# First batch of a cross-covariance attention with a max-out network: norms of q by one-column matmuls, and A^T W in parts of 128, 256 and 384 columns

One core of a Trainium2 chip. The metric is the device time of one execution in microseconds (us); lower is better.

## The reference

```python
# q, k, v: (4, 6144, 256), tau = 1
qn = q / (norm(q, axis=1) + 1e-6);  kn = k / (norm(k, axis=1) + 1e-6)
a = softmax(kn.transpose(0, 2, 1) @ qn / tau, axis=-1)     # (4, 256, 256)
x = (v @ a).reshape(24576, 256)
h = max(x @ w1, x @ w2, x @ w3)                            # d_ff = 768
out = h @ w_out
```

The product of q and k, q^T k, is called the gram. The kernel folds the small matrix A of each batch into the weights: it makes A^T W for three W once per batch ("ew products"), so that x is never formed. Then it works through 48 chunks of 512 rows of v: six "h blocks" of six matmuls each, a maximum of three on ACT and DVE, and the "o products" with the output weights.

## The kernel before

What the change and the argument touch (cuts marked):

```python
    def gram(b):                       # first batch only
        # ... k^T k for the norms of k while k lands ...
        for tp in range(NG // 2):
            for j in range(CC):
                PE.matmul(ps[j][:, 0:C], lhsT=qt[:, tsl, jsl], rhs=kt[:, tsl, :], ...)        # q^T k
                PE.matmul(ps[j][:, C:C + P], lhsT=qt[:, tsl, jsl], rhs=qt[:, tsl, jsl], ...)  # q^T q

    def softmax_t(ps, rkb):            # norm of q: the diagonal of q^T q
        for j in range(CC):
            DVE.tensor_tensor_reduce(out=scr, in0=ps[j][:, C:C + P], in1=ident, ..., accum_out=n2q[:, j:j + 1])
        # ... Ln, Exp, scaling, Exp ...

    # the loads, in this order on one queue: q, then
    load_v(0)
    for fp in range(d_ff // FT):       # FT = 256 columns
        load_w(fp)
    load_v(1)

    # the start of the program
    ps = gram(0)
    # ... six warm matmuls (on zeros, their result is not read) ...
    et = softmax_t(*ps)
    v_transpose_pe(0)                  # chunk 0 of v by PE
    rinv = aw_first(et, aw)            # columns 0:256 of A^T W
    v_transpose(1)                     # chunk 1 of v by a DMA transposition
    hold_loads(1)                      # POOL waits until that has landed
    POOL.dma_start(out=wo_sb, ...)     # only now: the output weights
    # ... chunk 0: h block 0, columns 256:512, h blocks 1 and 2, columns 512:768, h blocks 3 to 5
    # ... chunk 1: h block 0, h block 1, then the first o products (they read wo_sb)
```

## Time and profile before

574.09 us median of 4 runs (574.03 to 574.11).

| what | value | how to read it |
|---|---|---|
| span | 572.1 us | first to last instruction |
| PE, DVE, ACT, POOL busy | 97, 72, 54, 41% | PE is the bound over the whole |
| PE in 40 slices | below 9 tenths in the first two and the last | the start and the end are all there is to gain |

The lines of the chain and of the timeline that carry the start stand in the prediction. These are lines of the timeline of the kernel before (start, length, engine, line):

```profile
42.19 10.85 SPq L365 DMA_TRANSPOSE vt_sb<-v_sb  x2
...
45.36 0.83 POOL L483 DMA_DIRECT2D wo_sb<-in_moe_w_out_dram  x1
...
50.63 0.82 PE L409 MATMUL o_ps<-wo_sb,ht_sb 128*128 128x256 bf16 x6
```

and this is the answer for the tile of the output weights:

```profile
DMA to landing us min/median/max: 5.2/5.2/5.2
```

Chunk 1 of v lands and its transposition starts at 42.19; when that is done, POOL issues the output weights at 45.36; they land 5.2 us later (the landing event of the trace is at 50.54). The first o matmul starts at 50.63. PE did not wait, so no view of waits names this load. But it landed only 0.09 us ahead of its use.

### The profile page before, as it was taken

How to read it: one execution, taken by the hardware profiler on the slowest of the kernel's cores; microseconds unless marked ns; L12 is line 12 of the kernel's file. 1: busy time of each engine (PE TensorE's matmuls, PEld its weight loads, DVE VectorE, ACT ScalarE, POOL GpSimd, SP SyncE). 2: the span in 40 equal slices, each digit the busy share in tenths (PEclk: the TensorE clock that was granted, in tenths of full speed). 3: DMA queues.
4: the chain of work that ended last, by engine and by line, in shares of the span. 5: the costliest groups of instructions: out<-in, count | busy, mean ns of one | idle time of the engine just before them, and what ended most of it. 6: DMA issues, size and time to landing. Idle time of an engine off the chain costs nothing.

```text
span 572.1 us, 9442 instructions
## 1 busy us (share of the span) xinstructions
PE 553.9 (97%) x3349; PEld 330.7 (58%) x3350; DVE 411.1 (72%) x647; ACT 309.1 (54%) x539; POOL 235.1 (41%) x240
## 2 busy tenths in 40 slices
PE   3799999999999999999999999999999999999997
PEld 2665555555755555555575555555575555555566
DVE  0048777877577777777768777777868778778775
ACT  1044567677454576776545467767645444444443
POOL 2443357776730078776560048777750000000000
PEclk9999999999999999999999999999999999999999
DMA  9998998884598168984179339885437323132112
GB/s 143 106 146 129 136 237 126 159 135 116 99 107 160 56 107 158 134 148 110 57 128 151 99 81 140 148 141 98 124 86 154 75 75 109 56 103 64 56 55 76
DMA packets 76960, 65.64 MB, mean 115 GB/s; under 512 B 52464, under 2 KB 62576, under 8 KB 76784
## 3 DMA queue, kind: packets, MB, share of 16 engines
q0 software_dynamic: 19072, 26.48, 38.7%
q1 hardware_dynamic: 57696, 38.41, 23.7%
q8 instruction: 26, 0.43, 0.3%
q14 instruction: 22, 0.18, 0.1%
q10 hardware_dynamic: 144, 0.13, 0.1%
HBM read 78.64 MB, written 25.17 MB: 181 GB/s over the span
## 4 chain that ended last, share of the span: by engine, by line
PE 93%; DMA 5%; POOL 0%; issue 0%; DVE 0%; POOLq 0%
PE h_ps L389 65%; PE o_ps L409 22%; DMA q_sb<-in_q_dram 5%; PE gram L260 3%; PE ew_ps L311 3%; POOL k_sb L99 0%; PE o_ps L434 0%; PE ew_ps L335 0%; PE warm_ps L469 0%; PE vt_ps L372 0%; PE gram L177 0%; PE n_ps L215 0%; DVE ht_sb L395 0%; DVE o_sb L461 0%; PE n_ps L217 0%
## 5 line engine op out<-in xcount | busy, mean ns | idle before, releaser
L389 PE MATMUL h_ps<-vt_sb,aw_sb 128*128 128x512 bf16 (+1 forms) x1764 | 406.7, 375 | 0.1
L389 PEld LDWEIGHTS <-aw_sb 128*128 128x128 bf16 x1764 | 171.8, 98 | 161.3 <-DVE aw_sb L317 2.0
L394 DVE TENSOR_TENSOR s_mx<-h_ps,s_mx 128x512 bf16<-128x512 f32 (+1 forms) x294 | 198.7, 676 | 87.1 <-ACT s_mx L393 86.8
L393 ACT ACTIVATE s_mx<-h_ps 128x512 bf16<-128x512 f32 (+1 forms) x294 | 172.4, 587 | 124.9 <-PE h_ps L389 124.0
L395 DVE TENSOR_TENSOR ht_sb<-h_ps,s_mx 128x512 bf16<-128x512 f32 (+1 forms) x294 | 200.2, 681 | 31.4 <-PE o_ps L409 0.5
L203 POOL TENSOR_TENSOR acc<-acc,sq 128x768 f32<-128x768 f32 x90 | 147.6, 1651 | 70.5 <-ACT sq L197 61.6
L409 PE MATMUL o_ps<-wo_sb,ht_sb 128*128 128x256 bf16 x1128 | 153.9, 273 | 0.0
L409 PEld LDWEIGHTS <-ht_sb 128*128 128x128 bf16 x1128 | 110.4, 98 | 52.0
L412 ACT ACTIVATE o_sb<-o_ps 128x512 f32<-128x512 f32 x94 | 56.1, 597 | 85.3 <-PE o_ps L409 85.3
L110 POOL DMA_DIRECT2D v_sb<-in_v_dram x48 | 27.5, 578 | 37.7 <-DMA vt_sb<-v_sb 35.5
L197 ACT ACTIVATE sq<-q_sb 128x768 bf16<-128x768 fp8e4 x48 | 40.5, 845 | 0.0
L197 ACT ACTIVATE sq<-k_sb 128x768 bf16<-128x768 fp8e4 x48 | 40.1, 835 | 0.0
L200 POOL CAST acc<-sq 128x768 f32<-128x768 bf16 x6 | 4.9, 823 | 68.7 <-ACT sq L197 68.7
L102 POOL DMA_DIRECT2D q_sb<-in_q_dram x33 | 18.4, 564 | 5.1 <-DMA v_sb<-in_v_dram 4.1
L165 PE MATMUL kk<-k_sb 128*128 128x256 fp8e4 x48 | 7.5, 338 | 11.9 <-DVE k_sb L151 6.3
L99 POOL DMA_DIRECT2D k_sb<-in_k_dram x29 | 16.1, 555 | 3.1 <-DMA v_sb<-in_v_dram 1.2
L260 PE MATMUL gram<-k_sb,q_sb 128*128 128x512 fp8e4 x144 | 16.8, 277 | 0.0
L260 PEld LDWEIGHTS <-q_sb 128*128 128x256 fp8e4 x144 | 15.9, 136 | 0.6
L314 ACT ACTIVATE aw_sb<-ew_ps,rinv 128x384 bf16<-128x384 f32 (+1 forms) x24 | 13.2, 555 | 5.5 <-PE ew_ps L311 4.7
L311 PE MATMUL ew_ps<-w_sb,et 128*128 128x384 bf16 (+1 forms) x96 | 15.6, 313 | 0.0
L177 PE MATMUL gram<-k_sb,q_sb 128*128 128x512 fp8e4 x48 | 11.4, 332 | 2.6 <-DMA q_sb<-in_q_dram 2.4
L165 PEld LDWEIGHTS <-k_sb 128*128 128x256 fp8e4 x48 | 6.4, 182 | 12.9 <-DMA k_sb<-in_k_dram 6.6
(67 smaller groups left out, 112.9 us busy)
## 6 DMA issues: line engine op xcount, KB each, us to landing
out_dram<-o_sb SPq DMA_DIRECT2D x41, 512.0 KB, 2.9
v_sb<-in_v_dram POOLq DMA_DIRECT2D x48, 256.0 KB, 4.2
k_sb<-in_k_dram POOLq DMA_DIRECT2D x24, 192.0 KB, 6.0
q_sb<-in_q_dram POOLq DMA_DIRECT2D x24, 192.0 KB, 7.6
out_dram<-o_sb SPq DMA_DIRECT2D x13, 256.0 KB, 2.0
k_sb<-in_k_dram POOLq DMA_DIRECT2D x5, 256.0 KB, 10.8
w_sb<-in_moe_w_dram POOLq DMA_DIRECT2D x9, 128.0 KB, 5.7
kf<-in_k_dram SPq DMA_DIRECT2D x1, 1024.0 KB, 4.8
```

The lines of the kernel that those rows point to most:

```text
L102: POOL.dma_start(out=qk[b][0][:, g0:g0 + w, :], in_=q_r[b][:, g0:g0 + w, :])
L110: POOL.dma_start(out=t, in_=v_r[gi // NCH, gi % NCH])
L197: ACT.activation(out=sq, in_=src, func=AF.Square)
L203: POOL.tensor_tensor(out=acc, in0=acc, in1=sq, op=ALU.add)
L260: PE.matmul(g[:, j * C:(j + 1) * C], lhsT=qt[:, tsl, j * P:(j + 1) * P], rhs=kt[:, tsl, :], start=(tp == 0 and j == 0), stop=(tp == NG // ...
L311: PE.matmul(ew[:, :w], lhsT=et[:, j, ic * P:(ic + 1) * P], rhs=w_sb[m][:, j, fsl], start=(j == 0), stop=(j == CC - 1))
L389: PE.matmul(t.rearrange("p (t n) -> p t n", n=P), lhsT=aw[m][:, ic, fsl], rhs=vt[:, tsl, ic, :], start=(ic == 0), stop=(ic == CC - 1))
L393: ACT.activation(out=s_mx, in_=hp[0], func=AF.Copy)
L394: DVE.tensor_tensor(out=s_mx, in0=hp[1], in1=s_mx, op=ALU.max)
L395: DVE.tensor_tensor(out=ht, in0=hp[2], in1=s_mx, op=ALU.max)
L409: PE.matmul(st["ps"][:, half], lhsT=ht[:, fc, t * P:(t + 1) * P], rhs=wo_sb[:, fc, :], start=(fc == 0), stop=(fc == FC - 1))
L412: ACT.activation(out=st["o"][:, t - 1:t + 1, :].rearrange("p t d -> p (t d)"), in_=st["ps"], func=AF.Copy)
```

## The change

Its intent is to shorten the string of dependences between the last piece of q and the first h matmul. The norms of q come from squares (half on ACT, half on DVE), summed by matmuls against a column of ones. The first part of A^T W is half as wide, the second part is made inside the first h block, and the weights are loaded in the same parts. Chunk 0 of v goes through two PSUM banks instead of one, and there are two warm matmuls instead of six. Cut to its core:

```diff
-                PE.matmul(ps[j][:, C:C + P], lhsT=qt[:, tsl, jsl], rhs=qt[:, tsl, jsl], ...)
+            ACT.activation(out=a[:, 0:h, :], in_=ra, func=AF.Square)
+            DVE.tensor_tensor(out=d[:, 0:h, :], in0=rd, in1=rd, op=ALU.mult)
+                    PE.matmul(nq[:, j:j + 1], lhsT=t[:, r, j * P:(j + 1) * P], rhs=ones_c, ...)
...
-    FT = 2 * P
+    PARTS = ((0, P), (P, 3 * P), (3 * P, d_ff))
...
+        sums(0)
         products(0, (0, 1))
-        sums(0)
         sums(1)
-        DVE.reciprocal(out=rinv, in_=rs_ps[:, 0:CC])
         products(1, (0, 1))
         for j in range(CC):
             products(j, (2,))
+        DVE.reciprocal(out=rinv, in_=rs_ps[:, 0:CC])
...
+    def h_block_first(aw, et, rinv):     # for each m: two h matmuls, then four ew products of PARTS[1]
...
-    for i in range(6):
+    for i in range(2):                   # warm matmuls
...
-                    for fp in range(1, d_ff // FT):
-                        gaps[2 * fp - 2].append(lambda fp=fp: aw_part(et, rinv, aw, fp, FT))
+                    gaps[2].append(lambda: aw_part(et, rinv, aw, *PARTS[2]))
```

More of the change, by code (lines that the diff above doesn't have):

```diff
@@ L75 @@
     sq_pool = ctx.enter_context(tc.tile_pool(name="sq", bufs=4))
+    sqq_pool = ctx.enter_context(tc.tile_pool(name="sqq", bufs=3))
     sm = ctx.enter_context(tc.tile_pool(name="sm", bufs=2))
@@ L118 @@
     SP.dma_start(out=kf, in_=k_r[0][:, 0:HEAD, :])
-    for load, widths in ((load_k, [8] * 5), (load_q, [8] * 4 + [4, 4, 4, 2, 2])):
+    QW = [8] * 4 + [4, 4, 4, 2, 2]
+    for load, widths in ((load_k, [8] * 5), (load_q, QW)):
         g0 = HEAD if load is load_k else 0
@@ L128, with load_w @@
     w_sb = [consts.tile([P, CC, d_ff], BF16, name=f"w{i}_sb") for i in range(3)]
-    FT = 2 * P
-    def load_w(fp):
-        fsl = slice(fp * FT, (fp + 1) * FT)
+    PARTS = ((0, P), (P, 3 * P), (3 * P, d_ff))
+    def load_w(lo, hi):
         for wt, w in zip(w_sb, w_list):
-            POOL.dma_start(out=wt[:, :, fsl], in_=w.rearrange("(cc p) f -> p cc f", p=P)[:, :, fsl])
+            POOL.dma_start(out=wt[:, :, lo:hi], in_=w.rearrange("(cc p) f -> p cc f", p=P)[:, :, lo:hi])
     load_v(0)
-    for fp in range(d_ff // FT):
-        load_w(fp)
+    for part in PARTS:
+        load_w(*part)
     load_v(1)
@@ L154, with gram_first @@
     neg_ln_tau = -math.log(float(tau)) if float(tau) != 1.0 else 0.0
-    def gram(b):
-        qt, kt = qk[b]
+    def gram_first():
+        qt, kt = qk[0]
         kk = htile("kk")
@@ L170, in gram, with squares, columns @@
             DVE.tensor_tensor(out=dkm[:, jsl], in0=kk[:, jsl], in1=ident, op=ALU.mult)
-        ps = [xtile(f"gram{j}") for j in range(CC)]
-        for tp in range(NG // 2):
-            tsl = slice(2 * tp, 2 * tp + 2)
-            last = tp == NG // 2 - 1
-            for j in range(CC):
-                jsl = slice(j * P, (j + 1) * P)
-                PE.matmul(ps[j][:, 0:C], lhsT=qt[:, tsl, jsl], rhs=kt[:, tsl, :],
-                          start=(tp == 0), stop=last, perf_mode=DR, skip_group_check=True)
-                PE.matmul(ps[j][:, C:C + P], lhsT=qt[:, tsl, jsl], rhs=qt[:, tsl, jsl],
-                          start=False, stop=last, perf_mode=DR, skip_group_check=True)
-            if tp == 11:
+        g = xtile("gram")
+        nq = htile("nq")
+        def squares(g0, w):
+            h = w // 2
+            a = sqq_pool.tile([P, QW[0] // 2, C], BF16, name="sqa")
+            d = sqq_pool.tile([P, QW[0] // 2, C], BF16, name="sqd")
+            ra, rd = qt[:, g0:g0 + h, :], qt[:, g0 + h:g0 + w, :]
+            ACT.activation(out=a[:, 0:h, :], in_=ra, func=AF.Square)
+            DVE.tensor_tensor(out=d[:, 0:h, :], in0=rd, in1=rd, op=ALU.mult)
+            return [(t, r) for t in (a, d) for r in range(h)]
+        def columns(rows, first=False, last=False):
+            for n, (t, r) in enumerate(rows):
+                for j in range(CC):
+                    PE.matmul(nq[:, j:j + 1], lhsT=t[:, r, j * P:(j + 1) * P], rhs=ones_c,
+                              start=(first and n == 0 and j == 0), stop=(last and n == len(rows) - 1),
+                              skip_group_check=True)
+        g0 = 0
+        rows = None
+        for i, w in enumerate(QW):
+            if rows:
+                columns(rows, first=(i == 1))
+            for tp in range(g0 // 2, (g0 + w) // 2):
+                tsl = slice(2 * tp, 2 * tp + 2)
+                for j in range(CC):
+                    PE.matmul(g[:, j * C:(j + 1) * C], lhsT=qt[:, tsl, j * P:(j + 1) * P], rhs=kt[:, tsl, :],
+                              start=(tp == 0 and j == 0), stop=(tp == NG // 2 - 1), perf_mode=DR,
+                              skip_group_check=True)
+            rows = squares(g0, w)
+            g0 += w
+            if i == 2:
                 kb_ps = htile("kb_ps")
@@ L187, in gram @@
                 ACT.activation(out=rkb, in_=lnk, func=AF.Exp, scale=-0.5)
-        return ps, rkb
+        columns(rows, last=True)
+        return [g[:, j * C:(j + 1) * C] for j in range(CC)], rkb, nq[:, 0:CC]
     SQW = 3
@@ L276, in exp_t, with softmax_first @@
         return et
-    def softmax_t(ps, rkb):
-        n2q = sm.tile([P, CC], FP32, name="n2q")
-        scr = sm.tile([P, P], FP32, name="scr")
-        for j in range(CC):
-            DVE.tensor_tensor_reduce(out=scr, in0=ps[j][:, C:C + P], in1=ident, scale=1.0, scalar=0.0,
-                                     op0=ALU.mult, op1=ALU.add, accum_out=n2q[:, j:j + 1])
+    def softmax_first(gs, rkb, n2q):
         lnq = sm.tile([P, CC], FP32, name="lnq")
@@ L287, in softmax_t @@
         ACT.activation(out=rq, in_=lnq, func=AF.Exp, scale=-0.5, bias=neg_ln_tau)
-        return exp_t(scaled([ps[j][:, 0:C] for j in range(CC)], rkb), rq)
+        return exp_t(scaled(gs, rkb), rq)
     def alloc_aw():
@@ L302, in rowsums, with product, evacuate, aw_part @@
         return rinv
-    def aw_part(et, rinv, aw, fp, w):
-        fsl = slice(fp * w, (fp + 1) * w)
-        n = 0
+    def product(et, ew, m, ic, lo, hi, js=range(CC)):
+        for j in js:
+            PE.matmul(ew[:, :hi - lo], lhsT=et[:, j, ic * P:(ic + 1) * P], rhs=w_sb[m][:, j, lo:hi],
+                      start=(j == 0), stop=(j == CC - 1))
+    def evacuate(rinv, aw, ew, m, ic, lo, hi):
+        dst, src, r = aw[m][:, ic, lo:hi], ew[:, :hi - lo], rinv[:, ic:ic + 1]
+        if ic == 0:
+            ACT.activation(out=dst, in_=src, func=AF.Copy, scale=r)
+        else:
+            DVE.tensor_scalar_mul(out=dst, in0=src, scalar1=r)
+    def aw_part(et, rinv, aw, lo, hi):
         for m in range(3):
@@ L309, in aw_part @@
                 ew = htile("ew_ps")
-                for j in range(CC):
-                    PE.matmul(ew[:, :w], lhsT=et[:, j, ic * P:(ic + 1) * P], rhs=w_sb[m][:, j, fsl],
-                              start=(j == 0), stop=(j == CC - 1))
-                if n % 2 == 0:
-                    ACT.activation(out=aw[m][:, ic, fsl], in_=ew[:, :w], func=AF.Copy,
-                                   scale=rinv[:, ic:ic + 1])
-                else:
-                    DVE.tensor_scalar_mul(out=aw[m][:, ic, fsl], in0=ew[:, :w],
-                                          scalar1=rinv[:, ic:ic + 1])
-                n += 1
+                product(et, ew, m, ic, lo, hi)
+                evacuate(rinv, aw, ew, m, ic, lo, hi)
     def aw_first(et, aw):
@@ L324, in aw_first @@
         rs_ps = xtile("rs_ps")
-        parts = [(m, ic, htile("ew_ps")) for m in range(3) for ic in range(CC)]
+        ews = [(m, ic, htile("ew_ps")) for m in range(3) for ic in range(CC)]
         def sums(j):
@@ L332, in products @@
         def products(j, ms):
-            for m, ic, ew in parts:
+            for m, ic, ew in ews:
                 if m in ms:
-                    PE.matmul(ew[:, :FT], lhsT=et[:, j, ic * P:(ic + 1) * P], rhs=w_sb[m][:, j, 0:FT],
-                              start=(j == 0), stop=(j == CC - 1))
+                    product(et, ew, m, ic, *PARTS[0], js=(j,))
+        sums(0)
         products(0, (0, 1))
-        sums(0)
         sums(1)
-        DVE.reciprocal(out=rinv, in_=rs_ps[:, 0:CC])
         products(1, (0, 1))
@@ L344, in aw_first @@
             products(j, (2,))
-        for n, (m, ic, ew) in enumerate(parts):
-            if n % 2 == 0:
-                ACT.activation(out=aw[m][:, ic, 0:FT], in_=ew[:, :FT], func=AF.Copy, scale=rinv[:, ic:ic + 1])
-            else:
-                DVE.tensor_scalar_mul(out=aw[m][:, ic, 0:FT], in0=ew[:, :FT], scalar1=rinv[:, ic:ic + 1])
+        DVE.reciprocal(out=rinv, in_=rs_ps[:, 0:CC])
+        for m, ic, ew in ews:
+            evacuate(rinv, aw, ew, m, ic, *PARTS[0])
         return rinv
@@ L369, in v_transpose_pe @@
         vt = vt_tile(gi)
-        vt_ps = xtile("vt_ps", cols=TPC * C, dtype=BF16)
-        for i in range(TPC * CC):
-            PE.matmul(vt_ps[:, i * P:(i + 1) * P], lhsT=v_sb[:, i * P:(i + 1) * P], rhs=ident,
-                      is_transpose=True, start=(i == 0), stop=(i == CC * TPC - 1))
-        half = TPC * CC // 2
-        ps = vt_ps.rearrange("p (i n) -> p i n", n=P)
-        DVE.tensor_copy(out=vt[:, half:, :], in_=ps[:, half:, :])
-        ACT.activation(out=vt[:, :half, :], in_=ps[:, :half, :], func=AF.Copy)
+        n = TPC * CC
+        cut = 6
+        banks = [xtile("vt_ps", cols=TPC * C, dtype=BF16), ps_h.tile([P, TPC * C], BF16, tag="h", name="vt_ps2")]
+        for b, (lo, hi) in enumerate(((0, cut), (cut, n))):
+            for i in range(lo, hi):
+                PE.matmul(banks[b][:, i * P:(i + 1) * P], lhsT=v_sb[:, i * P:(i + 1) * P], rhs=ident,
+                          is_transpose=True, start=(i == lo), stop=(i == hi - 1))
+        pa, pb = (t.rearrange("p (i n) -> p i n", n=P) for t in banks)
+        DVE.tensor_copy(out=vt[:, 0:cut, :], in_=pa[:, 0:cut, :])
+        ACT.activation(out=vt[:, cut:n, :], in_=pb[:, cut:n, :], func=AF.Copy)
     def h_block(gi, aw, fc, tsl=slice(0, TPC)):
@@ L395, in h_block @@
         DVE.tensor_tensor(out=ht, in0=hp[2], in1=s_mx, op=ALU.max)
+    def h_block_first(aw, et, rinv):
+        vt = vts[0]
+        hp = []
+        ews = []
+        for m in range(3):
+            t = htile(f"h_ps{m}")
+            for ic in range(CC):
+                PE.matmul(t.rearrange("p (t n) -> p t n", n=P), lhsT=aw[m][:, ic, 0:P], rhs=vt[:, :, ic, :],
+                          start=(ic == 0), stop=(ic == CC - 1))
+            hp.append(t)
+            ews.append([htile("ew_ps") for ic in range(CC)])
+            for ic in range(CC):
+                product(et, ews[m][ic], m, ic, *PARTS[1])
+        s_mx = mx_pool.tile([P, CHUNK], BF16, name="s_mx")
+        ht = hts[0][:, 0, :]
+        ACT.activation(out=s_mx, in_=hp[0], func=AF.Copy)
+        for ic in range(CC):
+            evacuate(rinv, aw, ews[0][ic], 0, ic, *PARTS[1])
+        DVE.tensor_tensor(out=s_mx, in0=hp[1], in1=s_mx, op=ALU.max)
+        for ic in range(CC):
+            evacuate(rinv, aw, ews[1][ic], 1, ic, *PARTS[1])
+        DVE.tensor_tensor(out=ht, in0=hp[2], in1=s_mx, op=ALU.max)
+        for ic in range(CC):
+            evacuate(rinv, aw, ews[2][ic], 2, ic, *PARTS[1])
     def o_steps(gi):
@@ L463, in last_chunk @@
         SP.dma_start(out=dst[:, HT + 1, :], in_=o_sb[:, HT + 1, :])
-    ps = gram(0)
+    first = gram_first()
     warm_ps = htile("warm_ps")
-    for i in range(6):
-        PE.matmul(warm_ps, lhsT=ident, rhs=warm, start=(i == 0), stop=(i == 5))
-    et = softmax_t(*ps)
+    for i in range(2):
+        PE.matmul(warm_ps, lhsT=ident, rhs=warm, start=(i == 0), stop=(i == 1))
+    et = softmax_first(*first)
     v_transpose_pe(0)
@@ L512 @@
                 if b == 0:
-                    for fp in range(1, d_ff // FT):
-                        gaps[2 * fp - 2].append(lambda fp=fp: aw_part(et, rinv, aw, fp, FT))
+                    gaps[2].append(lambda: aw_part(et, rinv, aw, *PARTS[2]))
                 else:
-                    gaps[0].append(lambda: aw_part(et, rinv, aw, 1, FH))
+                    gaps[0].append(lambda: aw_part(et, rinv, aw, FH, d_ff))
             for s, f in enumerate(pending):
@@ L537 @@
             for fc in range(FC):
-                h_block(gi, aw, fc)
+                if gi == 0 and fc == 0:
+                    h_block_first(aw, et, rinv)
+                else:
+                    h_block(gi, aw, fc)
                 for f in gaps[fc]:
```

## The prediction

> **What bounds the kernel now.** I read the busy shares first: PE is busy 97% of a span of 572.1 us and nothing else is over 72%. The unprofiled time is 574.1 us, so about 2.0 us lie outside the span; I carry that over. In the 40 slices PE is below 9 tenths only in the first two and the last. All that the change touches runs once, in the first batch, so I went to the start of the chain of waits (start us, length us, what):
>
> ```profile
> 3.97 16.66 DMA q_sb<-in_q_dram
> 20.91 12.72 DMA q_sb<-in_q_dram
> 33.67 0.32 PE gram L177
> ...
> 34.29 1.24 PE warm_ps L469 x5
> 35.53 0.45 PE vt_ps L372 x8
> 35.98 0.61 PE ew_ps L335 x4
> 36.59 0.08 PE rs_ps L329 x4
> 36.67 0.89 PE ew_ps L335 x8
> 37.56 1.41 PE h_ps L389 x6
> 38.97 1.31 PE ew_ps L311 x12
> 40.28 2.66 PE h_ps L389 x12
> 42.94 1.31 PE ew_ps L311 x12
> 44.25 6.54 PE h_ps L389 x30
> ```
>
> Up to 33.67 the loads of q set the time: nothing that PE does before that counts, unless it runs late. From 37.56 to the end PE follows on PE almost without a gap. So the change can only act in two ways: on the 3.9 us between the last piece of q (33.67) and the first h matmul (37.56), and on what PE still has to do after that. The second view is the timeline of this stretch (start, busy time, engine, line):
>
> ```profile
> 25.85 0.42 PE L177 MATMUL gram<-k_sb,q_sb 128*128 128x512 fp8e4 x1
> ...
> 34.09 0.29 DVE L282 CUSTOM_DVE_ANT_0 scr<-gram,ident 128x128 f32<-128x128 f32 x1 [14.01 <-PE gram L179]
> ...
> 34.75 0.75 DVE L268 TENSOR_TENSOR e_in<-gram,rkb 128x256 f32<-128x256 f32 x2
> 34.87 0.20 ACT L286 ACTIVATE lnq<-n2q 128x2 f32<-128x2 f32 x1 [6.00 <-DVE n2q L282]
> ...
> 35.34 0.91 ACT L275 ACTIVATE et<-e_in,rq 128x256 bf16<-128x256 f32 x2
> ...
> 36.01 0.42 DVE L376 COPY vt_sb<-vt_ps 128x512 bf16<-128x512 bf16 x1 [0.51 <-PE vt_ps L372]
> ...
> 36.47 0.60 ACT L377 ACTIVATE vt_sb<-vt_ps 128x512 bf16<-128x512 bf16 x1 [0.23 <-DVE vt_sb L376]
> ...
> 36.70 0.17 DVE L341 RECIPROCAL rinv<-rs_ps 128x2 f32<-128x2 f32 x1 [0.27 <-PE rs_ps L329]
> 36.97 1.21 ACT L347 ACTIVATE aw_sb<-ew_ps,rinv 128x256 bf16<-128x256 f32 x3
> ```
>
> Read it as one string of dependences: last gram matmul, diagonal of q^T q (34.09), Ln (34.87), exponentials (35.34), row sums, reciprocal (36.70), first copies of A^T W (36.97), first h matmul (37.52). PE's twelve ew products fill 35.98 to 37.56 beside it, so string and PE end together. From there to the end of the eighth h block (50.80) PE takes 13.24 us; its pure work is 48 h matmuls of 0.216 (3.88 us for 18, in the chain's later rows) and 24 products of 0.109 (1.31 for 12), 12.98 us. So only 0.26 us of stalls are left there. DVE works nearly without a pause in this stretch (4.78 and 4.69 us of 5 in 40 to 45 and 45 to 50), so it is nearly a second bound: 1.39 us a block (maxima at 46.82, 48.21, 49.60), where PE needs 1.30.
>
> **What the Trainium skill says.** "TensorE: Matmul & The Clock Gate", Part 1: the array runs at half clock until about a window (3.4 us) of sustained activity, and falls back after an idle one. The trace agrees: from 20.67 each pair of gram matmuls takes 0.32 us, from 26.06 on it takes 0.17, though the granted clock reads 1.00 throughout; the k stage before, 1.25 us of work in each 2.45, never got the fast rate. Part 2 there, LDWEIGHTS: a weight load costs by its columns, whatever the moving width. The trace agrees for one-column matmuls: four loads with row sums take 0.26 us, 0.065 each. "PSUM — Partial Sum Buffer", the section on bank collisions: two engines must not be in one bank and quadrant at once, so the scheduler orders them. The trace agrees: ACT's half of the transposed v (36.47) waits for DVE's half (36.01 + 0.42). "DMA: Bandwidth & Descriptors", Specifications: below 512 B a transfer is not at line rate. The first weight part goes from runs of 512 B written to 256 B; the trace before cannot say what that costs.
>
> **The change part by part.**
> *Norms of q.* Removed: 48 q^T q matmuls, two diagonal reductions, about 0.75 us of DVE on the string. Added: squares of each piece, half on ACT and half on DVE, and 96 one-column matmuls. These, at 0.065, are 6.2 us of PE, and the removed matmuls at 0.056 (0.17 a pair less 0.11) are 2.7, all but the last few beside q's loads. Squares of a piece of eight rows are about 1.1 us on each engine (1024 elements; L197 takes 0.845 for 768), pieces come every 2.45 us: hidden. On the string only the last piece of two rows is left: square of 256 elements, about 0.4 us (0.845 less 512 elements at 1.2 per ns), 33.68 to 34.07; four columns from 34.14, and, as between row sums' first load (36.32) and reciprocal (36.70), 0.38 us to the reader: Ln at about 34.5 instead of 34.87. DVE scales the gram at about 34.1 instead of 34.75, so it does not bind. Exponentials 34.98 to 35.9 instead of 35.34 to 36.25. Gain 0.35 us.
>
> *First part of 128 columns, v's copies in two banks.* Products of 128 columns cost a weight load, 0.065, so twelve are 0.8 us instead of 1.31, and PE no longer sets the end; the string does: row sums 0.45 us behind the second exponential (36.25 to 36.70 before), reciprocal at 36.35. DVE's larger copy of v, 768 elements, is about 0.56 us from 35.7 and just done. Reciprocal to copy is 0.27: 36.62. A copy of 128 columns takes about 0.29 instead of 0.40. First h matmul at about 37.0 instead of 37.52: 0.5 us earlier. Six warm matmuls to two: nothing, they fill idle time.
>
> *What is only moved.* The 128 columns left out of part one come back: before, 24 products of 0.109 after the first h, 2.62 us; now twelve of 0.109 and twelve of about 0.1625 (384 columns), 3.27. That returns 0.65 us. Sum on PE: -0.5 + 0.65 = +0.15.
>
> *Stalls.* The order h, products, h, products in the first block saves the waits of the first h group (1.41 against 1.29) and perhaps all of the other stalls, -0.1 to -0.25. Against it: block two now needs the columns copied during block one, and DVE's last copy there ends at about 40.7, just when PE wants it: +0.1. Copies on DVE are nine before and after (about 0.29, 0.42, 0.55 in place of 0.42), so its load is unchanged.
>
> Sum: -0.5 + 0.65 - 0.2 + 0.1 = about +0.05, within my error of 0.4. I choose 574.0, a little under before: the retuned warm count and the uneven cut of v look like the work of someone who measured, and the estimate of the square is on the safe side.
>
> **Rivals.**
> 1. The clock does not rise. If one-column matmuls do not count as activity, the q stage is half active, like the k stage, and stays slow: 48 gram matmuls at 0.213 and 96 columns at 0.107 are 20.5 us from 20.67, so it ends near 41 instead of 34, plus a slow start of h: 580 to 583 us. Against it: PE would have no pause from 20.67 on, unlike the k stage. A milder form, four fewer warm matmuls letting the clock fall before h, would cost 1 to 2 us. Together 8%.
> 2. The string shortens more than I think (squares in 0.3 us, copies in 0.25) and DVE's stalls vanish: h starts at 36.7, 573.5 us. 30%.
> 3. DVE takes over in block one or two, or the small weight pieces land late (before, parts of 128 KB came at some 0.65 us each behind v; the third half part is wanted at 36.35): 574.5 us. 20%.
>
> **Range and chances.** The middle is the sum, the range of 8 in 10 runs from a full rival 2 with a little more to rival 3 with a margin: 573.3 to 574.8. Two per cent is 11.5 us; the whole stretch that can be gained is 3.9 us, and the worst case above is 9. So within 2% is nearly certain.
>
> **What would show it.** Pair rate of the gram: 0.11 apart by about 26 us; if 0.21 persists, rival 1. Ln of q at 34.5, exponentials at 35.0, reciprocal at 36.35, first h at 37.0: each checks a step. Products after the first h must sum to 3.27 us. The h matmuls from the start of the first block to the end of the eighth should take about 13.7 us; over 13.9 is rival 3, and the idle before the h weight loads names DVE's copy. After chunk one the chain should be the same, shifted by a constant. I am wrong if the q stage ends after 34.5, or if the later chunks differ.

## The result, and the profile after

Four runs of the changed kernel: 576.15, 574.27, 574.50 and 574.46 us, median 574.48; before 574.09. The ratio is 1.0013 (95% interval 0.9995 to 1.0032): the same within 2%. Ratios are the mean time of one kernel's fast runs over that of the other's of the same rounds, so this is not quite the ratio of the medians, and here it carries the one long run. The trace is of that long run: span 574.3 us, where the other three have 572.5 to 572.7. So its lateness has first to be told apart from what every run has. The run of the profile before took 573.92 us.

**The long run's own part.** Lines of POOL's timeline, first of the kernel before; POOL issues the next load when a piece of q has landed (in brackets: idle before, and what ended it):

```profile
15.79 0.28 POOL masks.py:199 TENSOR_SCALAR_AFFINE_SELECT ident<-ident 128x128 bf16<-128x128 bf16 x1 [11.04 <-issue]
...
23.37 0.53 POOL L110 DMA_DIRECT2D v_sb<-in_v_dram  x1 [1.93 <-DMA q_sb<-in_q_dram]
25.86 0.73 POOL L135 DMA_DIRECT2D w_sb<-in_moe_w_dram  x1 [1.96 <-DMA q_sb<-in_q_dram]
```

and of the changed kernel:

```profile
17.06 0.28 POOL masks.py:199 TENSOR_SCALAR_AFFINE_SELECT ident<-ident 128x128 bf16<-128x128 bf16 x1 [12.30 <-issue]
...
25.55 0.53 POOL L111 DMA_DIRECT2D v_sb<-in_v_dram  x1 [3.75 <-DMA q_sb<-in_q_dram]
27.97 0.73 POOL L137 DMA_DIRECT2D w_sb<-in_moe_w_dram  x1 [1.89 <-DMA q_sb<-in_q_dram]
```

The selection that builds the identity is 1.27 us late, before the first instruction of the change, the squares of the first piece at 21.00, has run. The second piece of q (23.37 against 25.55) is 2.18 us late; the third follows at the old distance. From 20 to 24 us the loads moved 0.43 MB before and 0.37 MB after. The packed trace holds every DMA packet, and they show where the time went: before, none of the 2 KB packets on the loads' queue in that stretch took more than 0.324 us; after, two that start at 20.76 and 20.83 took 2.05 and 1.91. Both start before the first square. The last piece starts its gram matmuls at 35.36 instead of 33.67, only 1.69 us late, because in the kernel before one of the later pieces came 2.05 us behind its neighbour, where the changed kernel needed 1.30. The other three runs have spans 1.6 to 1.8 us shorter than this one. I therefore read times from the last piece of q on. That the delay of q belongs to this run and not to the change is likely: the two packets started before anything of the new norms ran, though all of this is one trace.

**The string.** Timeline of the changed kernel, PE, then ACT and DVE:

```profile
35.36 0.43 PE L200 MATMUL gram<-k_sb,q_sb 128*128 128x512 fp8e4 x2
...
37.18 0.20 PE L351 MATMUL rs_ps<-ones_c,et 128*128 128x1 bf16 x2
...
37.58 0.20 PE L351 MATMUL rs_ps<-ones_c,et 128*128 128x1 bf16 x2
...
38.51 0.61 PE L425 MATMUL h_ps<-vt_sb,aw_sb 128*128 128x512 bf16 x2 [0.26 <-ACT aw_sb L332]
...
43.74 2.11 PE L326 MATMUL ew_ps<-w_sb,et 128*128 128x384 bf16 x12
45.69 6.78 PE L409 MATMUL h_ps<-vt_sb,aw_sb 128*128 128x512 bf16 x30
52.84 0.81 PE L455 MATMUL o_ps<-wo_sb,ht_sb 128*128 128x256 bf16 x6 [0.36 <-DMA wo_sb<-in_moe_w_out_dram]
```

```profile
36.18 0.17 ACT L306 ACTIVATE lnq<-nq 128x2 f32<-128x2 f32 x1 [0.34 <-PE nq L188]
...
36.62 0.91 ACT L300 ACTIVATE et<-e_in,rq 128x256 bf16<-128x256 f32 x2
```

```profile
37.82 0.17 DVE L365 RECIPROCAL rinv<-rs_ps 128x2 f32<-128x2 f32 x1
```

| us after the last gram piece starts (33.67 before, 35.36 after) | before | predicted | after |
|---|---|---|---|
| Ln of q's norms | 1.20 | 0.83 | 0.82 |
| first exponential | 1.67 | 1.31 | 1.26 |
| reciprocal | 3.03 | 2.68 | 2.46 |
| first h matmul | 3.85 | 3.35 | 3.15 |
| transposition of chunk 1 starts | 8.52 | not looked at | 8.98 |
| output weights issued | 11.69 | not looked at | 12.15 |
| output weights landed | 16.87 | not looked at | 17.43 |
| PE free for the first o matmul | 16.96 | 17.0 | 16.95 |
| first o matmul | 16.96 | as the row above | 17.48 |
| end of the span | 538.4 | 538.3 | 538.9 |

"PE free" after is worked out: the last group of h matmuls ends at 45.69 + 6.78 = 52.47; before it ended at 44.16 + 6.63 = 50.79 and the o products began 0.16 us ahead of that, as matmuls overlap; so 52.31 after. The predicted entry is the 16.96 of before and the prediction's sum for PE, +0.05. The predicted end is the predicted 574.0 less 2.0 us outside the span and less 33.67, rounded.

The string is 0.70 us shorter and the stretch from the first h matmul until PE is free is 0.69 us longer (13.11 to 13.80). They cancel. Of the 0.69, 0.64 are the products that were moved (3.26 us against 2.62). The rest is a difference of stalls, 0.13 us before and 0.17 after. Most of the 0.17 sits in the fourth h block, where the weight loads wait for DVE's copies of the 384-column products:

```profile
45.85 0.16 PEld L409 LDWEIGHTS <-aw_sb 128*128 128x128 bf16 x2 [0.22 <-DVE aw_sb L334]
...
46.37 0.11 PEld L409 LDWEIGHTS <-aw_sb 128*128 128x128 bf16 x2 [0.36 <-DVE aw_sb L334]
...
46.90 5.08 PEld L409 LDWEIGHTS <-aw_sb 128*128 128x128 bf16 x25 [0.41 <-DVE aw_sb L334]
```

Little of these 0.99 us reaches PE: two of the h matmuls there start 0.25 and 0.30 us after the one before instead of 0.216, 0.12 us in all. After the stretch PE does not go on: the o products start at 52.84, 0.53 us after PE is free. The line at 52.84 names the wait (its 0.36 us count from the modelled end of the matmul before). The chain of waits of the changed kernel says the same, read from the end:

```profile
38.23 6.10 DMA v_sb<-in_v_dram
44.32 0.02 issue
44.34 2.88 DMA vt_sb<-v_sb
47.22 0.06 issue
47.28 0.18 POOL guard L526
47.47 0.04 issue
47.51 5.29 DMA wo_sb<-in_moe_w_out_dram
52.79 0.04 issue
52.84 0.81 PE o_ps L455 x6
```

Before, the chain ran through PE from 33.67 to past 57 us. Now it runs through transfers until 52.79: chunk 1 of v, its transposition, POOL's wait for that, and the output weights. No matmul between 35 and 52 us is on it. The wait of 0.53 us accounts for the difference at the end (538.9 less 538.4), as PE reaches the o products at the same distance in both.

**Why the load came later.** Chunk 1 of v lands 0.46 us later after the last piece of q than before (8.98 less 8.52), and the output weights are issued later by the same 0.46; their own transfer took 0.1 longer (5.29 against 5.18), so they land 0.56 later. The landing events in the two traces, at the end of each transfer, are:

| landing, us | before | after |
|---|---|---|
| chunk 0 of v | 34.86 | 36.55 |
| nine weight pieces | every 0.674 on average, to 40.93 | three of 128 columns to 37.65 (0.367 each), three of 256 to 39.70 (0.683), two of 384 to 41.68 (0.99), the third at 43.07 (1.39) |
| chunk 1 of v | 42.18 | 44.32 |

Measured against 0.674 us for 256 columns, the small pieces took 0.09 us more in all (1.10 against 1.01), the middle ones 0.03, and the 384-column ones 0.34: the third 0.38 more, the two before it 0.04 less.

The packets of this stretch, from the landing of the last piece of q to that of chunk 1, tell more. Before, 2,381 packets of 512 and 2,048 B went through the loads' queue, and none of them took more than 1.5 times the usual time of its size (0.060 and 0.173 us). After, 39 of 1,885 did, the longest 0.735 us for 768 B, where 0.079 is usual. Together they took 6.9 us more than usual; spread over 16 DMA engines that is 0.43 us (an estimate), about the 0.46 us by which chunk 1 was late. So most of the lateness can be put down to long packets, and not to the number of pieces. Packets of 512 and 2,048 B, the sizes of the kernel before, were among them, as in the delay of q. Whether an ordinary run of the changed kernel has them too is not known; without them, the pieces would have cost some 0.1 us (0.09 and 0.03 as above, an estimate) and PE would have met the output weights almost on time.

A fetch of instructions shares the DMA engines at that time. These are lines of the transfers of the changed kernel from 40 to 42 us (queue, kind: packets, MB, share of the 16 engines):

```profile
q0 software_dynamic: 415, 0.34, 116.4%
q8 instruction: 1, 0.02, 3.0%
```

Before, the fetch that comes next to this place is at 44.79, after chunk 1 had landed. That the changed program, with more instructions at its start, fetches earlier and holds up the piece is a guess that the traces allow, no more. Of the earlier fetches, that at 29.30 in the kernel before stands beside the piece of q that came 2.05 us behind its neighbour, and that at 30.40 in the changed kernel beside pieces that came on time, 1.30 us apart. And long packets of weights began at 36.04, before the fetch at 40.27. A disturbance of this one run, which had others, is the rival that the packets speak for.

### The profile page after: what moved, and what is told of

Same layout as the page of the kernel before. It is cut to its first block, busy times and chain, and to the rows that moved or that the text cites. A ratio compares the mean times of both kernels' runs of the same rounds, so it can differ in the third digit from the quotient of the medians.

```text
span 574.3 us, 9556 instructions
## 1 busy us (share of the span) xinstructions
PE 553.8 (96%) x3394; PEld 328.7 (57%) x3394; DVE 418.7 (73%) x652; ACT 315.6 (55%) x548; POOL 235.2 (41%) x240
## 4 chain that ended last, share of the span: by engine, by line
PE 90%; DMA 6%; issue 2%; POOL 1%; DVE 0%; POOLq 0%
PE h_ps L409 63%; PE o_ps L455 21%; DMA v_sb<-in_v_dram 3%; PE gram L285 3%; PE ew_ps L326 2%; DMA q_sb<-in_q_dram 1%; DMA wo_sb<-in_moe_w_out_dram 1%; DMA vt_sb<-v_sb 1%; POOL k_sb L100 0%; PE o_ps L480 0%; POOL w_sb L137 0%; POOL q_sb L103 0%; PE n_ps L240 0%; DVE ht_sb L415 0%; DVE o_sb L507 0%
## 5 line engine op out<-in xcount | busy, mean ns | idle before, releaser
L181 ACT ACTIVATE sqa<-q_sb 128x1024 bf16<-128x1024 fp8e4 (+2 forms) x9 | 6.9, 770 | 20.6 <-DMA q_sb<-in_q_dram 19.8
L332 ACT ACTIVATE aw_sb<-ew_ps,rinv 128x384 bf16<-128x384 f32 (+2 forms) x27 | 14.5, 545 | 6.1 <-PE ew_ps L326 5.0
L326 PE MATMUL ew_ps<-w_sb,et 128*128 128x384 bf16 (+2 forms) x108 | 17.6, 308 | 0.0
L285 PE MATMUL gram<-k_sb,q_sb 128*128 128x512 fp8e4 x144 | 16.8, 277 | 0.0
L334 DVE TENSOR_SCALAR aw_sb<-ew_ps,rinv 128x384 bf16<-128x384 f32 (+2 forms) x27 | 13.9, 564 | 0.7 <-PE ew_ps L326 0.6
```

The lines of the kernel that those rows point to most:

```text
L285: PE.matmul(g[:, j * C:(j + 1) * C], lhsT=qt[:, tsl, j * P:(j + 1) * P], rhs=kt[:, tsl, :], start=(tp == 0 and j == 0), stop=(tp == NG // ...
L326: PE.matmul(ew[:, :hi - lo], lhsT=et[:, j, ic * P:(ic + 1) * P], rhs=w_sb[m][:, j, lo:hi], start=(j == 0), stop=(j == CC - 1))
```

## The experiments

None gave a result. The first four, close variants of the two kernels, were returned once because no chip ran them, and the second time refused before the chip: "it sets a matmul performance mode (perf_mode, DoubleRow and the like), which is held for now". All four keep the gram's DoubleRow mode of the kernels. They were:

The changed kernel, unedited, for a profile of an ordinary run.

> The changed kernel again, unedited, for a profile of an ordinary run and for how often the 576 us run comes. Theory A (the load of the output weights sets the first o products): time 574.3 to 574.6, last q piece at about 33.7 as before, and the first o matmul starts within 0.1 us of the landing of the output weights, with PE idle just before it. Theory B (the extra products and DVE's copies after the first h matmul cost it): no idle before the first o matmul; the h blocks one to eight take 13.9 us or more. Theory C (squares or one-column matmuls slow q's loads in every run): the last q piece lands at 34.5 or later here too, and runs of about 576 come often.

The changed kernel with the output weights' load moved:

```diff
     wo_sb = consts.tile([P, FC, d_model], BF16, name="wo_sb")
+    POOL.dma_start(out=wo_sb, in_=moe_w_out.rearrange("(fc p) d -> p fc d", p=P))
...
     hold_loads(1)
-    POOL.dma_start(out=wo_sb, in_=moe_w_out.rearrange("(fc p) d -> p fc d", p=P))
```

> The changed kernel with the load of the output weights issued right behind the second chunk of v instead of behind its transposition; nothing else moved. Theory A: the wait of the first o products goes, and the time falls to 574.0 or below (573.5 to 574.0). Theory B: stays at 574.3 to 574.6, as nothing waited for that load.

The same edit in the kernel before.

> The kernel before with the same move of the output weights' load. Theory A: in the kernel before the load lands (45.36 + 5.2 = 50.6) just as PE arrives (50.63), so it gains at most 0.1 us: 574.0 to 574.1. If it gains more, PE was waiting there already unseen. Any kernel may lose if the load now collides with the transposition of v.

And the kernel before with the weight loads alone in the new parts:

```diff
-    def load_w(fp):
-        fsl = slice(fp * FT, (fp + 1) * FT)
+    PARTS = ((0, P), (P, 3 * P), (3 * P, d_ff))
+    def load_w(lo, hi):
```

> The kernel before with only its weight loads cut into column parts of 128, 256 and 384; products still in three parts of 256. Theory A with costly small pieces: the second chunk of v lands 0.3 to 0.6 us later than 42.19, its transposition and the output weights follow, PE waits at the first o products, and the time is 574.3 to 574.6. If the cut costs the transfers nothing: 574.1 and landing at 42.2.

I then wrote stand-ins without the mode. A plain matmul over both rows of each pair would double the number of gram matmuls, and PE is already busy for 3.99 of the 4 us from 24 to 28 in the kernel before; it could become the bound while q lands, which is another regime. So the stand-ins multiply every second row only. That keeps the count of matmuls, their output columns, the loads and the waits, and gives a wrong result:

```diff
-            tsl = slice(2 * tp, 2 * tp + 2)
+            row = 2 * tp
-                    PE.matmul(..., lhsT=qt[:, tsl, ...], rhs=kt[:, tsl, :], ..., perf_mode=DR, ...)
+                    PE.matmul(..., lhsT=qt[:, row, ...], rhs=kt[:, row, :], ...)
```

No chip ran them. The expectations of the full set:

> The kernel before with its q and k products as plain matmuls over every second row (matmuls that set a performance mode could not be submitted any more): wrong numbers on purpose, the same count of matmuls, columns, loads and waits. It is the base for the other stand-ins. If it stands for the kernel before: 573.8 to 574.4 us, last q piece at about 33.7, first h matmul at about 37.5, output weights landing at about 50.6.

> The changed kernel with the same stand-in for its gram. Theory A (the load of the output weights sets the first o products): 0.2 to 0.6 us slower than the stand-in of before, last q piece as there, and the first o matmul starts within 0.1 us of the landing of the output weights, with PE idle just before it. Theory B (the extra products and DVE's copies after the first h matmul cost it): no idle before the first o matmul; from the first h matmul to the end of the eighth block 13.9 us or more. Theory C (squares or one-column matmuls slow q's loads in every run): the last q piece lands 0.5 us or more later than in the stand-in of before.

> The stand-in of the changed kernel with the load of the output weights issued right behind the second chunk of v instead of behind its transposition; nothing else moved. Theory A: the wait of the first o products goes, and the time falls by 0.3 us or more below the stand-in of the changed kernel, to the stand-in of before or under it. Theory B: no change, as nothing waited for that load.

> The stand-in of before with only its weight loads cut into column parts of 128, 256 and 384; products still in three parts of 256. Theory A with costly small pieces: the second chunk of v lands 0.3 to 0.6 us later than in the stand-in of before, its transposition and the output weights follow, PE waits at the first o products, and it is 0.2 to 0.5 us slower. If the cut costs the transfers nothing: same time and same landing.

What follows from this section is only what is not known. No edit has taken the wait away, so that the output weights set the end is read from one trace and its chain, not tested. Whether they do so in an ordinary run, and whether the change or a disturbed run made them late, is open. No version that could beat both kernels has been run; the one to try first is the changed kernel with the output weights' load moved.

## Why the prediction was right or wrong

- **Within 2%**: right, and nearly certain from the start, as only the first 50 us are touched.
- **The step that failed**: "the change can only act in two ways", on the string and on what PE still has to do. There was a third: the transfers behind the weights. The prediction read that from 37.56 PE follows on PE "almost without a gap" and took it as proof that nothing else was near. The output weights landed 0.09 us ahead of their first use. In the trace after, they land late and PE waits 0.53 us. Rival 3 came nearest (574.5 us, late transfers), but it looked for them at the weight pieces before the first h matmul, not 14 us later.
- **The loads of q** were taken as the same in every run ("Up to 33.67 the loads of q set the time"). In the run of the trace they ended 1.69 us later, and no term or rival of the prediction had such a run. Its own sign, "wrong if the q stage ends after 34.5", came true, though not by the clock that rival 1 named. This and the wait make the 2.2 us by which the traced span is longer. The 576.15 us of this run lie 1.35 us above the top of the range; the other three times lie inside.
- **Norms of q**: right on the string. Ln came 0.82 us behind the last piece; 0.83 was predicted. One cost was far too high without harm: a one-column matmul was put at 0.065 us, from four weight loads that take 0.26 together. In the trace after, groups of eight start 0.21 us apart (31.59 and 31.80), 0.026 each. The 96 cost about 2.5 us of PE (an estimate), not 6.2.
- **First part of A^T W**: the mechanism was right and the size low. The first h matmul came 0.70 us earlier relative to q, where 0.5 was predicted. The term that was mis-sized is the row sums: "0.45 us behind the second exponential". Measured: the second exponential ends at 36.62 + 0.91 = 37.53 and the reciprocal starts at 37.82, 0.29. Before, all four row sums stood behind four products and started at 36.43, 0.18 us after the second exponential; now two of them are done before it ends and the other two start 0.05 us after it. That this order made the difference fits, and was not tested alone.
- **What is moved returns**: right. 0.65 was predicted for the products, and 0.64 measured.
- **Stalls**: the wrong sign. The two terms, -0.2 and +0.1, say 0.1 us less; PE lost about 0.05 more. The 0.26 us of stalls that the prediction saw were about half the modelled tail of the last matmul: from the first h start to the first o start PE took 13.11 us for 12.98 of work, so only 0.13 was there to save. The stall that it feared in block two did not come; the one behind the 384-column copies came in block four. By the prediction's own measure, to the modelled end of the eighth block, 13.7 us were predicted and 13.96 measured, over its line of 13.9 for rival 3.
- **PE arrives as predicted, in part by luck**: the string was 0.2 us shorter and the stretch 0.14 longer than predicted, and these errors cancel: 16.95 us after the last piece against 17.0.
- **The middle was put low** by the thought that someone had tuned this. The sum of the terms was +0.05; the inclination had nothing in the profile behind it.
- **The clock (rival 1)** did not happen: groups of eight gram matmuls take 1.97 us at 21.02 and at 25.31, 1.55 at 27.73 and 1.09 at 30.18, so the fast rate came in time. The reason given against it did not hold: PE did pause, for 1.89 us before 25.31. And its 20.5 us rested on 0.107 us for a column; the groups at 27.07 and 27.35, before the fast rate, start 0.28 us apart for eight, 0.035 each.
- **What stays open.** Whether the three ordinary runs wait in the same place: their times lie 0.2 to 0.4 us over the median before, and their spans 0.4 to 0.6 over the traced one. A shorter or equal wait would fit, but they have no trace here. Whether the long packets, which account for most of the 0.46 us, come with the change, with the earlier fetch of instructions, or with this run alone. And why two packets of q took some 2 us, which goes with most of the rest of the 576.15 us.

## What to carry to other kernels

When the engine that bounds a kernel is to arrive earlier, look at every transfer that it will use next and write down how long each has been landed: a load that arrives just in time appears in no list of waits and takes over as soon as the engine is early or the load is late. Subtract work that is only moved before counting a gain: here 0.70 us gained, 0.64 of it given back by moved products and 0.05 by stalls. If the only trace is of the longest run, align both traces at a common event before comparing them, and where a load comes late, compare packets of one size in both traces before the change is blamed.

## What the Trainium skill lacked or had wrong

- "DMA: Bandwidth & Descriptors", Specifications, asks for at least 512 B for line rate. In the trace after, weight pieces written in runs of 256 B landed every 0.367 us for 64 KB, against 0.337 for half of a piece in runs of 512 B in the trace before: 9% more time. The row gives no figure of the loss; the page's section "Why small descriptors are slow" works out 27% overhead for a descriptor of 256 B, but none for 512 B beside it.
- "TensorE: Matmul & The Clock Gate", Part 1, does not say whether one-column matmuls count as activity. Here gram and one-column matmuls alternated and the fast rate came between the group at 25.31 (1.97 us for eight) and that at 30.18 (1.09 us); whether the columns helped is not separated.
- No page that I read on tracing warns that a transfer which lands just before its use is in no list of waits; here the margin was 0.09 us.
